# Repeated weight loads that pad every attention segment to three instruction pages

## The chip, the cores and the metric

The kernel runs on one core of one Trainium2 chip. Its time is the device time of that core in microseconds; three executions of the kernel before took 1864.36, 1864.82 and 1868.08 us, and the median, 1864.82 us, is what the changed kernel is compared with. The profiled execution took 1870.9 us.

A core has engines with instruction streams of their own. Here PE is the matrix engine (TensorE). It runs two kinds of instruction that matter: a weight load (LDWEIGHTS, shown as PEld), which puts the stationary operand into the array, and a matmul, which streams the moving operand through it. DVE is the vector engine, ACT the activation engine, POOL and SP further ones.

## The reference

Four layers follow each other on 2048 rows of 512 numbers: attention with a recurrent memory, a gated MLP, and the same two again, each with a layer norm before it and the residual added after it. What matters here is the attention, which goes over 64 segments of 32 rows, one after the other:

```python
mem = mem0                                        # 8 rows of memory
for s in range(n_seg):                            # 64 segments of 32 rows
    xs = x[:, s * seg_len:(s + 1) * seg_len, :]
    h = jnp.concatenate([mem, xs], axis=1)        # 40 rows of 512
    q = jnp.einsum('btd,dhe->bhte', h, Wq)        # 32 heads of 128
    k = jnp.einsum('btd,dhe->bhte', h, Wk)
    v = jnp.einsum('btd,dhe->bhte', h, Wv)
    scores = jnp.einsum('bhqe,bhke->bhqk', q, k) * scale
    scores = jnp.where(mask[None, None], scores, -1000000000.0)
    p = _softmax(scores, axis=-1)
    o = jnp.einsum('bhqk,bhke->bhqe', p, v)
    o = jnp.einsum('bhte,hed->btd', o, Wo)
    mem = o[:, :M, :]                             # the memory of the next segment
    outs.append(o[:, M:, :])
```

A segment needs the memory that the one before it leaves, so the 128 segments of the two attention layers form a chain.

## The kernel before

All work of a segment on PE is a fixed list. Two helpers issue most of it. `mm_chunk` makes 16 matmuls of 512 columns (4 steps of the contraction `kt`, in each 4 column groups `cg` of 32 columns that work side by side in the array), each with its own weight load; the program therefore holds 32 instructions per chunk. `wo_pass` makes 128 matmuls of 128 columns, which is 256 instructions.

```python
def mm_chunk(ps, lhs, rhs, kts=range(KT)):
    for kt in kts:
        for cg in range(4):
            nc.tensor.matmul(ps[32 * cg:32 * cg + 32, :], lhsT=lhs(kt, cg), rhs=rhs(kt, cg),
                             start=(kt == 0), stop=(kt == KT - 1), tile_position=(0, 32 * cg))

def wo_pass(po, lhs, heads=range(H)):
    for h in heads:
        n = h // 8 * 8 + 2 * (h % 4) + h // 4 % 2
        for cg in range(4):
            nc.tensor.matmul(po[32 * cg:32 * cg + 32, 0:128], lhsT=lhs[:, n, :], rhs=wo_rhs(h, cg),
                             start=(h == 0), stop=(h == H - 1), tile_position=(0, 32 * cg))
```

The order inside a segment, with the parts that are not on PE cut away (... marks a cut):

```python
def segment(s, fill, spare1, spare2, tail):
    ...
    r0 = qk(0)                    # one mm_chunk, then ScalarE copies PSUM to r0
    r2 = qk(2)
    qk_T(0, r0)                   # VectorE turns the rows
    r1 = qk(1)
    qk_T(2, r2)
    r3 = qk(3)
    qk_T(1, r1)
    ...
    scores(0)                     # 32 small matmuls for both score halves together
    qk_T(3, r3)
    ...
    v_mm(0, psV[0][:, 0, :])      # one mm_chunk
    fill()
    close(0)
    nc.vector.tensor_copy(VA[:, 0]..., psV[0][:, 0, :])
    scores(1)                     # needs qk_T(3)
    close(1)
    ...
    v_mm(1, psV[1][:, 0, :])
    fill()
    ...                           # psM: 4 matmuls
    pv(0)
    pv(1)                         # 32 matmuls for both
    ...                           # psD: 8 matmuls
    fill()
    ...
    wo_pass(pw, uT_cur)           # 128 matmuls
    ...
    build_hA(s + 1, pw)           # the next segment's input, from pw
    ...
    fill()
```

`fill()` takes the next piece of work that has no hurry and puts it where PE would wait: in the segments with `s % 4` of 1, 2 and 3 a part of the projections of the block of 128 rows to come (8, 8, 16 and 32 instructions in the four places of a segment), in those with `s % 4 == 0`, from the fifth block on, a part of an output projection (2, 2, 4 and 8 instructions). Without the fills a segment is 600 instructions on PE: 128 for the four qk chunks, 64 for the two v chunks, 64 for the scores, 8 for psM, 64 for pv, 16 for psD and 256 for the Wo pass.

Of the kernel before, what the change touches and what calls it, by code (L numbers as in the profile page):

```python
# [16 lines left out]
KT = 4  # L17
# [6 lines left out]
FF = 1376  # L24
FH = 688
LN_EXP_SET = 6
FCH = [(0, 128), (128, 128), (256, 128), (384, 128), (512, 128), (640, 48)]
ORDERED = {mybir.EngineType.PE, mybir.EngineType.DVE, mybir.EngineType.Activation}

# [75 lines left out]
def _ln_exp_table(nc):  # L105

    nc.scalar.add_instruction(mybir.InstLoadActFuncSet(name=nc.get_next_instruction_name(), engine=mybir.EngineType.Activation,
                                                       act_func_set_id=LN_EXP_SET, ins=[], outs=[]))

# [114 lines left out]
def b_block(tc, c, rows, front, xd, MV_out, RS_out, w_sp, w_out, S, first, out_final=None):  # L224
# [4 lines left out]
    with ExitStack() as ctx:  # L229
# [116 lines left out]
        def turn_u(t):  # L346
            pT = one.tile([P, 1024], BF16, name="pT")
            for fc, (f0, fsz) in enumerate(FCH):
                nc.tensor.transpose(pT[0:fsz, fc * P:(fc + 1) * P], u[t][:, f0:f0 + fsz], ident_bf[:])
# [4 lines left out]
        def finish(t):  # L354
            py = one.tile([P, DM], F32, name="py")
            for fc, (f0, fsz) in enumerate(FCH):
                nc.tensor.matmul(py[:], lhsT=uT[t][0:fsz, fc, :], rhs=w_out_sb[0:fsz, fc, :], start=(fc == 0), stop=(fc == 5))  # L357
# [33 lines left out]
def kernel(  # L391
# [55 lines left out]
    for blk in range(2):  # L447
        a_block(tc, c, rows, front, MV[0], RS[0], MV[1], RS[1], wqkv, A_Wo, S, first=(blk == 0))
        b_block(tc, c, rows, front, xd, MV[0], RS[0], B_w_sp, B_w_out, S, blk == 0, out_final=out2 if blk == 1 else None)
# [26 lines left out]
def a_block(tc, c, rows, front, MV_in, RS_in, MV_out, RS_out, wqkv, Wo, S, first):  # L476
    nc = tc.nc
    NSEG = S // SEG
    NB = S // P
# [3 lines left out]
    with ExitStack() as ctx:  # L483
# [33 lines left out]
        def qk_rhs(j, kt, cg):  # L517
            W_sb = Wq_sb if j < 2 else Wk_sb
            return W_sb[:, kt, :].rearrange("p (r gs i eb el) -> p r eb i gs el", r=2, gs=4, i=4, eb=4)[:, j % 2, cg]

        def v_rhs(r, kt, cg):
            return Wv_sb[:, kt, 2048 * r + 512 * cg:2048 * r + 512 * cg + 512]
# [1 line left out]
        def wo_rhs(h, cg):  # L524
            return Wo_sb[:, h, :].rearrange("p (kt g el) -> p g kt el", kt=4, g=4)[:, cg]

        def mm_chunk(ps, lhs, rhs, kts=range(KT)):

            for kt in kts:
                for cg in range(4):  # L530
                    nc.tensor.matmul(ps[32 * cg:32 * cg + 32, :], lhsT=lhs(kt, cg), rhs=rhs(kt, cg),  # L531
                                     start=(kt == 0), stop=(kt == KT - 1), tile_position=(0, 32 * cg))

# [23 lines left out]
        def b_units(tb, early=False):  # L557
            bs = blk_state[tb]

            for k, j in enumerate((0, 2, 1, 3, 4, 5)):  # L560
                ps = (accA if k % 2 == 0 or not early else accB).tile([P, 512], F32, name="psb")
                for kts in (((0,), (1,), (2, 3)), ((0, 1, 2, 3),))[k % 2]:
                    mm_chunk(ps, lambda kt, cg: bs["hB"][:, kt, :],
                             lambda kt, cg: qk_rhs(j, kt, cg) if j < 4 else v_rhs(j - 4, kt, cg), kts)
                    if kts[-1] != KT - 1:
                        yield

                def out(j=j, ps=ps):
                    if j >= 4:
                        nc.scalar.copy(bs["VB"][:, j - 4].rearrange("p i e -> p (i e)"), ps[:])  # L570
                        return
                    r = rowp.tile([P, 512], BF16, name="rowsB", bufs=2)
                    nc.scalar.copy(r[:], ps[:])  # L573
                    turns.append(lambda: nc.vector.transpose(
                        out=bs[("QTB", "KTB")[j // 2]][:, j % 2].rearrange("p a b -> p (a b)"), in_=r[:]))

                copies.append(out)
                yield
# [65 lines left out]
        def store_o(s, pw, eng):  # L644
# [2 lines left out]
            nc.scalar.copy(o_sb[:], pw[:, 0:128])  # L647
            eng.dma_start(o_d[SEG * (s - 1):SEG * s, :].rearrange("r (cg c) -> cg r c", cg=4), o_sb[:])

        def segment(s, fill, spare1, spare2, tail):  # L650
            tb, j4 = s // 4, s % 4
            st = seg_state.pop(s)
            QQ, KTB, VB = st["QQ"], st["KTB"], st["VB"]
            KA = KAr[s % 2]
            VA = vsp.tile([P, 2, 4, DH], BF16, name="VA")
            hA_cur = hA[s % 2]
# [5 lines left out]

            def qk(j):
                ps = (accB if j < 2 else accA).tile([P, 512], F32, name="psm")
                mm_chunk(ps, lambda kt, cg: hA_cur[:, kt, :], lambda kt, cg: qk_rhs(j, kt, cg))
                r = rowp.tile([P, 512], BF16, name="rows", tag="rowsQK", bufs=4)
                nc.scalar.copy(r[:], ps[:])  # L667
                return r
# [2 lines left out]
                nc.vector.transpose(out=QQ[:, j % 2, :, 0:32] if j < 2 else KA[:, j % 2], in_=r[:])  # L671

            def v_mm(r, ps):
                mm_chunk(ps, lambda kt, cg: hA_cur[:, kt, :], lambda kt, cg: v_rhs(r, kt, cg))

            def ends(q):

# [43 lines left out]
            def tok_out(r):  # L721
# [4 lines left out]
                                        in1=Rr[:, :, :, 24:32], op=ALU.mult)  # L726

            r0 = qk(0)
            r2 = qk(2)
            qk_T(0, r0)  # L730
# [3 lines that stand above are left out]
# [3 lines left out]
            qk_T(3, r3)  # L737
            psV = [attO[r].tile([P, 2, 512], F32, name="psV") for r in range(2)]
            v_mm(0, psV[0][:, 0, :])
            fill()  # L740
            close(0)
            nc.vector.tensor_copy(VA[:, 0].rearrange("p i e -> p (i e)"), psV[0][:, 0, :])
            scores(1)
            close(1)
            spare1()
            v_mm(1, psV[1][:, 0, :])
            fill()
            nc.scalar.copy(VA[:, 1].rearrange("p i e -> p (i e)"), psV[1][:, 0, :])  # L748
# [56 lines left out]
        for s in range(NSEG):  # L805
# [21 lines left out]
            def tail():  # L827
# [11 lines left out]
                if due and (j4 != 3 or tb + 2 >= NB):  # L839
                    ys.append(due.pop(0))  # L840
                    rows.y_load(ys[0], first, nc.sync)

            segment(s, lambda: next(more, None), spare1, spare2, tail)
        pw = accB.tile([P, 512], F32, name="pw")
        wo_pass(pw, uT[NSEG % 2])
# [47 lines left out]
```

The softmax here doesn't subtract the row's maximum and nothing guards it: scores larger than these inputs give would overflow.

## Time and profile before

| | |
|---|---|
| time, median of 3 | 1864.82 us |
| span of the profiled execution | 1870.9 us |
| PE busy | 1745.0 us (93%) |
| weight loads busy (overlap the matmuls) | 1007.2 us (54%) |
| DVE / ACT busy | 1156.5 us (62%) / 1112.3 us (59%) |
| PE instructions in the built program | 87,231 (43,596 weight loads, 43,596 matmuls, 39 others) |

In the views below a line of a group reads: source line, engine, operation, output and inputs by the program's names, shape, count; then busy time in us and the mean duration of one in ns; then the idle time of the engine just before them, and what ended most of it. "issue" stands where an engine waited for nothing that the profile shows. The chain of waits is the work that ended last, followed back from the end of the kernel; its lines read start, length, what.

An instruction takes 64 bytes, and the profile lists the transfers that bring instructions to the engines as a queue of their own: for one queue 340 packets and 5.57 MB, so 16.4 KB each, which is 256 instructions. The text calls such a packet a page, and the place in an instruction stream where one page ends and the next begins a page edge.

### The profile page before, as it was taken

What the parts mean: (1) busy time and instruction counts of PE and PEld (TensorE: products, weight loads), DVE (VectorE), ACT (ScalarE), POOL (GpSimd) and SP (SyncE); (2) the same over time, 40 slices, a digit from 0 to 9 for tenths busy, and PEclk for the clock granted to TensorE, in tenths of its full rate; (3) what the DMA queues carried; (4) which work ended last, traced back from release to release, by engine and by line L of the source; (5) the groups of instructions that cost most, each with busy time, mean ns of one, the idle gap of its engine ahead of it and who ended that gap; (6) DMA issues with size and microseconds to landing.
All of it is one profiled execution on the core that took longest, in us unless ns stands there. A gap on an engine that the chain in (4) does not pass through costs nothing.

```text
span 1870.9 us, 94288 instructions
## 1 busy us (share of the span) xinstructions
PE 1745.0 (93%) x43572; PEld 1007.2 (54%) x43596; DVE 1156.5 (62%) x2700; ACT 1112.3 (59%) x2074; POOL 137.1 (7%) x289
## 2 busy tenths in 40 slices
PE   2999999999999999889989999999999999998898
PEld 1555555555555555545545555555555555554455
DVE  1666666676667666674446666666766676665822
ACT  1666666766666666562036666666666666665600
POOL 5000000000000000032010000000000000001200
PEclk8999999999999999999989999999999999999999
DMA  9100000021002111277940000001210121114685
GB/s 348 48 19 20 20 19 17 20 72 38 19 16 71 42 26 37 80 159 166 206 134 21 21 21 21 22 21 32 80 35 21 28 88 39 29 47 112 155 181 135
DMA packets 189267, 125.80 MB, mean 67 GB/s; under 512 B 135896, under 2 KB 164328, under 8 KB 188872
## 3 DMA queue, kind: packets, MB, share of 16 engines
q1 hardware_dynamic: 167016, 71.01, 16.1%
q0 software_dynamic: 10560, 34.07, 5.6%
q10 hardware_dynamic: 11296, 14.70, 2.6%
q8 instruction: 340, 5.57, 1.2%
q14 instruction: 55, 0.45, 0.1%
HBM read 59.29 MB, written 33.56 MB: 50 GB/s over the span
## 4 chain that ended last, share of the span: by engine, by line
PE 85%; DMA 5%; DVE 4%; issue 3%; ACT 2%; POOL 1%; SPq 0%; ACTq 0%; DVEq 0%; POOLq 0%
PE psm L531 24%; PE pw L586 12%; PE psV L531 12%; PE psb L531 9%; PE pg L329 7%; PE psS L688 5%; PE psO L711 4%; PE pwB L598 4%; PE py L357 2%; PE psD L763 2%; DMA Wo_sb<-in_A_Wo_dram 2%; PE pz L263 1%; PE psM L753 1%; DMA uT<-u 1%; PE psM L754 1%
## 5 line engine op out<-in xcount | busy, mean ns | idle before, releaser
L531 PEld LDWEIGHTS <-hA 128*32 128x32 bf16 x12288 | 305.5, 96 | 316.9 <-DVE hA L642 47.8
L667 ACT CAST rows<-psm 128x512 bf16<-128x512 f32 x512 | 300.1, 586 | 198.4 <-PE psm L531 198.4
L586 PE MATMUL pw<-Wo_sb,uT 128*32 128x128 bf16 x16640 | 267.0, 220 | 40.6 <-issue 31.5
L531 PE MATMUL psm<-Wq_sb,hA 128*32 128x512 bf16 x4096 | 277.6, 384 | 12.8 <-DVE hA L642 9.3
L586 PEld LDWEIGHTS <-uT 128*32 128x32 bf16 x16640 | 236.1, 97 | 88.9 <-DVE uT L773 47.8
L531 PE MATMUL psm<-Wk_sb,hA 128*32 128x512 bf16 x4096 | 272.3, 382 | 0.5 <-ACT rowsB L573 0.5
L531 PE MATMUL psV<-Wv_sb,hA 128*32 128x512 bf16 x4096 | 268.0, 382 | 0.0
L671 DVE STREAM_TRANSPOSE QQ<-rows 128x512 bf16<-128x512 bf16 x256 | 182.0, 711 | 88.8 <-ACT rows L667 87.7
L723 DVE TENSOR_TENSOR uT<-psO,Rt 128x384 bf16<-128x384 f32 x256 | 138.5, 541 | 119.2 <-ACT Rt L779 119.0
L692 ACT ACTIVATE E<-psS 128x448 bf16<-128x448 f32 x256 | 139.9, 547 | 117.8 <-PE psS L688 117.8
L671 DVE STREAM_TRANSPOSE KA<-rows 128x512 bf16<-128x512 bf16 x256 | 181.8, 710 | 40.4 <-ACT rows L667 38.9
L773 DVE TENSOR_TENSOR uT<-psO,Rm 128x128 bf16<-128x128 f32 x256 | 62.4, 286 | 163.7 <-PE psD L763 163.7
L779 ACT ACTIVATE Rt<-Rt 128x512 f32<-128x512 f32 x256 | 157.4, 629 | 4.1
L329 PE MATMUL pg<-z2n,wspT 128*128 128x344 bf16 x1024 | 154.8, 309 | 1.0 <-DVE u L337 1.0
L688 PEld LDWEIGHTS <-KA 128*64 128x64 bf16 x2048 | 79.8, 113 | 106.0 <-DVE KA L671 105.2
L771 ACT ACTIVATE Rt<-psD 128x1024 f32<-128x1024 f32 x128 | 131.2, 1025 | 6.0
L531 PEld LDWEIGHTS <-hB 128*32 128x32 bf16 x3072 | 77.8, 97 | 97.0 <-issue 25.4
L329 PEld LDWEIGHTS <-wspT 128*128 128x128 bf16 x1024 | 97.9, 98 | 54.2 <-issue 7.8
L695 DVE TENSOR_TENSOR E<-E,maskN 128x448 bf16<-128x448 bf16 x256 | 95.2, 372 | 41.7 <-ACT E L692 41.7
L531 PE MATMUL psb<-Wq_sb,hB 128*32 128x512 bf16 x1024 | 89.9, 391 | 26.2 <-DVE hB L546 26.2
L688 PE MATMUL psS<-QQ,KA 128*64 128x80 bf16 x2048 | 109.9, 208 | 1.1
L748 ACT CAST VA<-psV 128x512 bf16<-128x512 f32 x128 | 75.0, 586 | 56.5 <-PE psV L531 56.5
(147 smaller groups left out, 2216.1 us busy)
## 6 DMA issues: line engine op xcount, KB each, us to landing
Wo_sb<-in_A_Wo_dram POOLq DMA_DIRECT2D x8, 1024.0 KB, 13.6
xs<-xd ACTq DMA_DIRECT2D x32, 256.0 KB
o_d<-o_sb SPq DMA_DIRECT2D x126, 64.0 KB
y_o<-o_d SPq DMA_DIRECT2D x24, 256.0 KB
xd<-y_o SPq DMA_DIRECT2D x22, 256.0 KB
Wq_sb<-in_A_Wq_dram POOLq DMA_DIRECT2D x8, 512.0 KB, 6.8
Wk_sb<-in_A_Wk_dram POOLq DMA_DIRECT2D x8, 512.0 KB, 10.7
Wv_sb<-in_A_Wv_dram POOLq DMA_DIRECT2D x8, 512.0 KB, 11.4
```

Source lines behind the costliest of these rows:

```text
L329: nc.tensor.matmul(pg[t][:, k, 0:344], lhsT=wsp[t][:, st, :], rhs=z2n[:, st, 344 * k:344 * k + 344], start=(st == 0), stop=(st == NT - 1))
L531: nc.tensor.matmul(ps[32 * cg:32 * cg + 32, :], lhsT=lhs(kt, cg), rhs=rhs(kt, cg), start=(kt == 0), stop=(kt == KT - 1), tile_position=(0, ...
L586: nc.tensor.matmul(po[32 * cg:32 * cg + 32, 0:128], lhsT=lhs[:, n, :], rhs=wo_rhs(h, cg), start=(h == 0), stop=(h == H - 1), tile_position ...
L667: nc.scalar.copy(r[:], ps[:])
L671: nc.vector.transpose(out=QQ[:, j % 2, :, 0:32] if j < 2 else KA[:, j % 2], in_=r[:])
L688: nc.tensor.matmul(pS[64 * g:64 * g + 64, i, c0:80 if K is KA else 112], lhsT=K[:, r, n:n + 2, :].rearrange("p h k -> p (h k)"), rhs=q if ...
L692: nc.scalar.activation(out=E[:, r], in_=pS, func=ACT.Exp, scale=scale)
L695: nc.vector.tensor_tensor(out=E[:, r], in0=E[:, r], in1=maskN[:, j4, :].unsqueeze(1).to_broadcast([P, 4, 112]), op=ALU.mult)
L723: nc.vector.tensor_tensor(out=hview(uT_nxt[:], r, 8, 32), in0=oview(r, 8, 32), in1=Rr[:, :, :, 0:24], op=ALU.mult)
L748: nc.scalar.copy(VA[:, 1].rearrange("p i e -> p (i e)"), psV[1][:, 0, :])
L771: nc.scalar.activation(out=Rt[:], in_=psD[:], func=ACT.Ln)
L779: nc.scalar.activation(out=rt, in_=rt, func=ACT.Exp, scale=-1.0)
```

## The change

The changed kernel issues weight loads a second, third, ... time, with the same weights and no matmul of their own, until every segment is 768 PE instructions long: 3 pages of 256. As a Wo pass has 256 instructions, every Wo pass contains exactly one page edge; before, its place moved from segment to segment, because a segment of 600 instructions and its fills is not a whole number of pages. With 768 it stays at the same place. The loads go before the 16 matmuls of `qk(3)` and of `v_mm(0)`, spread evenly, half in each chunk. `again_of` counts them: 168 less the fills that lie between this Wo pass and the one before it, so 104 in the segments with `s % 4` of 2 and 3, 136 (or 128) in the others, and up to 168 in a layer's last block, which has hardly any fills; the first segment of each layer gets fewer, by `FILL_AHEAD`, which sets where the edge falls. In the built program every Wo pass inside the chain of segments has it at the same place, about 97 instructions in.

```diff
+PE_PAGE = 256
+SEGMENT_PE = 600
+FILL_AHEAD = ((0, 0, 0, 98), (0, 0, 0, 95))
...
-        def mm_chunk(ps, lhs, rhs, kts=range(KT)):
+        def mm_chunk(ps, lhs, rhs, kts=range(KT), again=0):
 
             for kt in kts:
                 for cg in range(4):
+                    k = 4 * kt + cg
+                    for _ in range(again * (k + 1) // 16 - again * k // 16):
+                        nc.tensor.ldweights(lhs(kt, cg), tile_position=(0, 32 * cg))
                     nc.tensor.matmul(ps[32 * cg:32 * cg + 32, :], lhsT=lhs(kt, cg), rhs=rhs(kt, cg),
                                      start=(kt == 0), stop=(kt == KT - 1), tile_position=(0, 32 * cg))
...
+        def fills_of(s):
+
+            if s < 0:
+                return FILL_AHEAD[not first]
+            if s % 4 == 0:
+                return (2, 2, 4, 8) if s // 4 > 3 else (0, 0, 0, 0)
+            return (8, 8, 16, 32) if s // 4 + 1 < NB else (0, 0, 0, 0)
+
+        def again_of(s):
+
+            return 3 * PE_PAGE - SEGMENT_PE - fills_of(s - 1)[3] - sum(fills_of(s)[:3])
+
         def segment(s, fill, spare1, spare2, tail):
             tb, j4 = s // 4, s % 4
+            again = again_of(s)
...
-                mm_chunk(ps, lambda kt, cg: hA_cur[:, kt, :], lambda kt, cg: qk_rhs(j, kt, cg))
+                mm_chunk(ps, lambda kt, cg: hA_cur[:, kt, :], lambda kt, cg: qk_rhs(j, kt, cg), again=again // 2 if j == 3 else 0)
...
-                mm_chunk(ps, lambda kt, cg: hA_cur[:, kt, :], lambda kt, cg: v_rhs(r, kt, cg))
+                mm_chunk(ps, lambda kt, cg: hA_cur[:, kt, :], lambda kt, cg: v_rhs(r, kt, cg), again=again - again // 2 if r == 0 else 0)
```

In the built program that is 15,167 weight loads more (58,763 in place of 43,596), 102,398 PE instructions in place of 87,231. Two more things stand there that the diff does not show: each extra load increments PE's semaphore, and in the two chunks that hold extra loads each of the 16 matmuls does so too, where before only the last one of a chunk did. No other engine's work changes.

## The prediction

> **What bounds the kernel now.** I read the page first, then the chain of waits in one stretch, then all that the Wo line waits for, then the timeline of one segment.
>
> ```profile
> PE 1745.0 (93%) x43572; PEld 1007.2 (54%) x43596; DVE 1156.5 (62%) x2700; ACT 1112.3 (59%) x2074; POOL 137.1 (7%) x289
> ...
> q8 instruction: 340, 5.57, 1.2%
> ...
> PE 85%; DMA 5%; DVE 4%; issue 3%; ACT 2%; POOL 1%; SPq 0%; ACTq 0%; DVEq 0%; POOLq 0%
> ...
> L531 PEld LDWEIGHTS <-hA 128*32 128x32 bf16 x12288 | 305.5, 96 | 316.9 <-DVE hA L642 47.8
> ...
> L688 PEld LDWEIGHTS <-KA 128*64 128x64 bf16 x2048 | 79.8, 113 | 106.0 <-DVE KA L671 105.2
> ```
>
> PE carries 85% of the chain; no other engine or DMA comes near. 3% of the chain, 56 us of 1870.9, is "issue": PE had nothing to wait for and yet did nothing. Two passes of the chain show what that is:
>
> ```profile
> 646.33 1.68 PE pw L586 x119
> 648.01 0.90 issue
> 648.92 0.34 PE pw L586 x9
> ...
> 658.62 1.90 PE pw L586 x128
> ```
>
> One Wo pass stops for 0.90 us after 119 of its 128 matmuls, another runs through in 1.90 us. The pass's own view says how often:
>
> ```profile
> L586 PEld LDWEIGHTS <-uT x16640: 92/97/150, 52.8 to 1713.1; 128*32 128x32 bf16 x199
> ...
>   issue: 72.3, 91
> ```
>
> (72.3 us counts loads and matmuls, so most stalls twice.) Laying the program's PE list beside the trace's weight-load starts explains it. Gaps over 300 ns that no semaphore accounts for lie at instruction 194 or 195 and whole multiples of 256 after it: page edges. In Wo passes whose edge is 0 to 168 instructions in, the loads take 1.70 us from first to last, always; beyond about 170 nearly all stop at the edge. Counted over the attention, 65 stalls hold up the loads for 61 us in all: 43 in Wo passes (41 us), 22 in the qk chunks just after one (20 us). Where the edge before was under 2.3 us away, so that waiting surely ended the interval (26 cases), edge to resumption took 2.3 to 4.0 us, mean 3.1, spread 0.4. So a page needs about 3.1 us after the previous edge, and edges closer in time than that cost the difference. A Wo pass eats a page in 1.7 us; a qk chunk takes 0.87 us for 32 instructions.
>
> The segments agree: the stretch from one Wo pass to the next takes at best 11.30, 11.23, 11.10 and 11.10 us for the four segments of a block, and 0.5 us more on average. Between stalls PE is saturated; nothing else is to be had.
>
> **What the Trainium skill says.** "Runtime: NRT & Kernel Launch", section Instruction fetch mechanics: instructions come in 16 KiB blocks of 256, fetched while the current one runs, and the cost of an edge is "mostly hidden". The block size agrees (5.57 MB over 340 packets); "hidden" fails where 256 instructions take under 3 us. "TensorE: Matmul & The Clock Gate", section LDWEIGHTS (loading the stationary operand), gives columns / 1.2 ns, so 27 ns for 32 columns; the trace contradicts it: a Wo pass does 128 such loads in 1.80 us, 14 ns each, and 64 columns take 113 ns against 96, so 17 ns for 32 columns more. The same page, section The mechanism, says loads are pulled ahead of running matmuls; the trace agrees (loads for the next step begin 2 ns after the matmul whose weights they replace). The same page, section The cost: per-tile semaphore tail, says that increments of a semaphore serialise at 26.3 ns each. Nothing in the trace of before shows it, since only one matmul of a chunk increments there.
>
> **The change part by part.**
>
> Removed: up to 56 us of stalls. New stalls: with 768 instructions a segment has three edges, where before it had about 2.6. I placed the new edges on the clean timing of before (extra loads at no time): from Wo to the qk chunks 3.85 or 4.42 us, from there into scores(1), or the fills and loads just before it, mostly 3.54 or 3.51 us, but 3.09 us in 22 segments and 2.0 to 2.9 us in some 20 (first and last blocks of a layer), and from there to the next Wo edge mostly 3.71 us. Against 3.1 +- 0.4 us the 22 cost 0.2 us each (4 us), the 20 some 0.5 (10), all others a few hundredths (6): 20 us. Net gain 56 - 20 = 36 us, so 1829 us if the extra loads are free.
>
> Added, the loads: 15,167 / 128 = 118 a segment, 59 in each of two chunks, 15 in each step of 216 ns beside the four that belong there. At the Wo pass's 14 ns, 19 loads need 266 ns, 50 ns over the 216 of the matmuls. Times 4 steps, 2 chunks and 128 segments: 51 us. This is a lower bound on the load path's rate, since in a Wo pass the matmuls (128 columns, 56 ns for a group of four) set the pace as well; loads for different column groups start 3 to 4 ns apart, and two loads of one group have been 15 ns apart at the start of a chunk. With 15 ns inside a group and 3.4 ns between groups a chunk with 52 extra loads just fits, one with 64 to 68 is 150 to 210 ns over: about 26 us. I take 30 us, and 1859 us in all.
>
> Added, the increments: 59 + 16 = 75 in a chunk of 0.87 us. At 26.3 ns they take 1.97 us. The signal that qk(3) is ready would come some 0.9 us late, and it has no slack:
>
> ```profile
> 664.02 1.05 PE L531 MATMUL psm<-Wk_sb,hA 128*32 128x512 bf16 x16
> ...
> 665.11 0.59 ACT L667 CAST rows<-psm 128x512 bf16<-128x512 f32 x1 [0.28 <-PE psm L531]
> ...
> 665.73 0.71 DVE L671 STREAM_TRANSPOSE KA<-rows 128x512 bf16<-128x512 bf16 x1 [0.15 <-ACT rows L667]
> ...
> 666.24 0.39 PE L531 MATMUL psb<-Wq_sb,hB 128*32 128x512 bf16 x4
> ...
> 666.56 0.11 PEld L688 LDWEIGHTS <-KA 128*64 128x64 bf16 x2 [0.42 <-DVE KA L671]
> ```
>
> The last qk chunk ends at 665.07; the ACT copy, the DVE transpose (to 666.44) and the second score loads at 666.56 follow at once, while PE has just finished its fill. 0.9 us late is 0.9 us lost, 118 us over 128 segments, so 1829 + 118 = 1947 us.
>
> **The rivals.**
>
> (1) Loads are nearly free: repeated loads overlap the streaming matmuls, increments do not queue. About 1829 us. For it: loads run ahead by design, the four groups accept them 3 to 4 ns apart, and chunk steps leave 200 of 216 ns without a load. Against: repeated loads of one group without a matmul between occur nowhere in this trace.
>
> (2) The load path fills up, increments do not matter: 1845 to 1885 us, my central case. The fetch gain is mostly handed back.
>
> (3) The increments queue, or a repeated load has to wait for the matmul that still uses the array: a new wait takes the place of the removed one, at scores(1) or inside the two chunks. 1900 to 1980 us for the increments. For it: the skill's figure and the tight chain above. If each repeated load waited for the whole of the one before it (96 ns), 118 of them would be 11 us a segment and the time would nearly double; against that speak loads of one group 15 ns apart.
>
> **Range and chances.** I give (1) 0.2, (2) 0.45, (3) 0.35. Even (1) lands near 1829, while 2% faster begins at 1827.5 and needs the residual stalls to be hidden too; so faster gets 0.14. Within 2% (to 1902) takes the rest of (1), all of (2): 0.48. Slower 0.38. The middle of this is 1860 us; 8 times in 10 I expect 1820 to 1980.
>
> **What would show each step right or wrong.** Wo passes: all should run through in 1.70 us of loads, with no "issue" in them; a single stall of 0.5 us or more in most passes would mean I have the edge or its mechanism wrong. "issue" on the chain should fall from 3% to about 1%. The fetch queue should carry some 399 packets. qk(3) and v_mm(0): their 16 matmuls should start over 0.65 us (3 steps of 216 ns) if loads are hidden, 0.8 to 1.1 us in case (2). Case (3) would show as ACT's copy of qk(3) starting late after the chunk's last matmul, or as PE weight loads at scores(1) waiting for DVE KA far over 0.42 us. Wrong in everything would be a fetch that depends on anything but the time since the last edge, such as other DMA traffic, or a chunk that slows several times over.

## The result, and the profile after

| | before | after |
|---|---|---|
| median of the comparison | 1865.62 us (4 runs) | 2098.56 us (4 runs, 2090.28 to 2101.63) |
| ratio, 95% interval | 1 | 1.1232 [1.1202, 1.1262] |
| first to last Wo pass, layers 1 and 2 | 732.9 and 737.5 us | 841.2 and 841.5 us |
| the rest of the profiled execution | 400.5 us | 405.9 us |

The change makes the kernel 12% slower, 233 us. The profiled execution after took 2088.6 us; 212 of its 218 us over before lie in the two attention stretches.

The page after, the same rows as before (column meanings are the same; the program's lines have moved, L531 is now L537, L586 is L592 and L688 is L707; the added loads are L536):

```profile
PE 1946.2 (93%) x43572; PEld 1372.9 (66%) x58763; DVE 1162.5 (56%) x2700; ACT 1109.9 (53%) x2074; POOL 137.3 (7%) x289
...
q8 instruction: 400, 6.55, 1.3%
...
PE 57%; ACT 11%; DVE 11%; PEld 10%; issue 7%; DMA 3%; SPq 1%; POOL 0%; ACTq 0%; DVEq 0%; POOLq 0%
...
L686 ACT CAST rows<-psm 128x512 bf16<-128x512 f32 x512 | 300.2, 586 | 377.6 <-PE L536 262.6
...
L536 PEld LDWEIGHTS <-hA 128*32 128x32 bf16 x15167 | 357.1, 93 | 23.3
...
L690 DVE STREAM_TRANSPOSE KA<-rows 128x512 bf16<-128x512 bf16 x256 | 181.8, 710 | 230.5 <-ACT rows L686 229.6
```

PE is as busy as before by share (93%), yet its part of the chain fell from 85 to 57%: ACT and DVE have come onto it. The ACT copies of the qk chunks now idle for 262.6 us until an added weight load (L536) lets them go, and the transpose behind them for 229.6 us. A row that puts ACT's wait down to a weight load shows that the loads' increments go to the semaphore on which ACT waits.

"issue" on the chain rose from 3 to 7%, where the prediction said about 1%. These are not page stalls: in the changed kernel the chain runs over the weight loads of the qk chunks, and the time between the loads of one step and the next, in which the matmuls go on, counts as "issue":

```profile
708.33 0.11 issue
708.44 0.11 PEld L537 x4
708.54 0.11 issue
```

What the change was meant to do in the Wo passes, it did. The Wo line's own view after:

```profile
L592 PEld LDWEIGHTS <-uT x16640: 92/97/97, 53.5 to 1928.8; 128*32 128x32 bf16 x199
...
  issue: 6.3, 8
```

"issue" ahead of Wo's loads and matmuls went from 72.3 us to 6.3 us; of the Wo passes of the attention one stalls, where 43 did.

The timeline of one segment (start us, length, engine, what; in brackets the idle time before it and its releaser) shows the price:

```profile
710.81 1.19 PE L537 MATMUL psm<-Wk_sb,hA 128*32 128x512 bf16 x16
...
712.58 1.69 PE L537 MATMUL psV<-Wv_sb,hA 128*32 128x512 bf16 x16
...
713.21 0.59 ACT L686 CAST rows<-psm 128x512 bf16<-128x512 f32 x1 [1.58 <-PE L536]
...
713.83 0.71 DVE L690 STREAM_TRANSPOSE KA<-rows 128x512 bf16<-128x512 bf16 x1 [1.46 <-ACT rows L686]
...
714.59 0.11 PEld L707 LDWEIGHTS <-KA 128*64 128x64 bf16 x2 [0.44 <-DVE KA L690]
...
715.66 0.55 ACT L711 ACTIVATE E<-psS 128x448 bf16<-128x448 f32 x1 [1.43 <-PE psS L707]
```

qk(3) ends at 712.00. Before, ACT's copy followed within 0.04 us; here it starts 1.21 us after that end, and the transpose (which turns the rows into KA) and the second score loads wait for it. That is the signal the prediction spoke of, 0.3 us later still than it said. A second late signal it did not speak of: ACT takes up the second scores (E, L711) 1.07 us after their first load, 714.59 to 715.66. In the segment of before that the prediction shows, that was 0.49 us, from 666.56 to

```profile
667.05 0.54 ACT L692 ACTIVATE E<-psS 128x448 bf16<-128x448 f32 x1 [0.91 <-PE psS L688]
```

The third thing is that v_mm(0) itself takes 1.69 us where a chunk took 1.05. The starts of PE's instructions show how (loads in ns of the trace; own and added loads together, matmuls left out):

```
qk(3), at first:   710809 710817 710824 710826 710832 710840 710841 710847 710855 710856 710862 710863 710871
qk(3), at the end: 711364 711394 711424 711454 711488 711518 711548 711578 711608
v_mm(0):           712602 712632 712662 712696 712726 712756 712786 712820 712850 712880 712910
```

The first loads of qk(3) follow each other by 1 to 8 ns. After some 55 increments, 0.55 us into the chunk, one goes out in 30 ns (34 where a matmul stands between), and v_mm(0) begins at that pace. So increments do not just arrive late: they hold back the loads and matmuls that carry them.

The trace also records when each increment of PE's semaphore takes effect. In the whole execution they follow each other by 30 ns 15,167 times, which is the number of the added loads, and by 34 or 35 ns 3,970 times; the matmuls have 3,840 increments more than before. At 711.36 us, when the hold sets in, 58 increments had been issued since the first added load and 10 had come out, so 48 had been let ahead. Those of qk(3) are all out at 713.18 us, just before ACT's copy, and those of v_mm(0) at 715.45 us; that of the second scores follows at 715.64, and ACT starts on them at 715.66. So both late signals stand in one row of increments. (In v_mm(0) the hold begins with only 25 outstanding, and at 713.2 us, when those of qk(3) are out, some 25 loads go out fast once more; why is open.)

### The profile page after: what moved, and what is told of

It is laid out like the page before. It is cut to its first block, busy times and chain, and to the rows that moved or that the text cites. A ratio compares the mean times of both kernels' runs of the same rounds, so it can differ in the third digit from the quotient of the medians.

```text
span 2088.6 us, 109455 instructions
## 1 busy us (share of the span) xinstructions
PE 1946.2 (93%) x43572; PEld 1372.9 (66%) x58763; DVE 1162.5 (56%) x2700; ACT 1109.9 (53%) x2074; POOL 137.3 (7%) x289
## 4 chain that ended last, share of the span: by engine, by line
PE 57%; ACT 11%; DVE 11%; PEld 10%; issue 7%; DMA 3%; SPq 1%; POOL 0%; ACTq 0%; DVEq 0%; POOLq 0%
PE psm L537 13%; PE psS L707 9%; PE pg L332 7%; PE psV L537 7%; PE pw L592 5%; PEld L537 4%; PEld L536 4%; PE psO L730 4%; ACT Rt L790 3%; ACT E L711 3%; PE psb L537 3%; PE pwB L604 3%; DVE E L714 2%; PE py L360 2%; DVE KA L690 2%
## 5 line engine op out<-in xcount | busy, mean ns | idle before, releaser
L537 PEld LDWEIGHTS <-hA 128*32 128x32 bf16 x12288 | 501.8, 94 | 195.7 <-DVE hA L648 50.6
L686 ACT CAST rows<-psm 128x512 bf16<-128x512 f32 x512 | 300.2, 586 | 377.6 <-PE L536 262.6
L537 PE MATMUL psV<-Wv_sb,hA 128*32 128x512 bf16 x4096 | 382.9, 381 | 0.3
L536 PEld LDWEIGHTS <-hA 128*32 128x32 bf16 x15167 | 357.1, 93 | 23.3
L537 PE MATMUL psm<-Wk_sb,hA 128*32 128x512 bf16 x4096 | 309.7, 381 | 0.5 <-ACT rowsB L579 0.5
L690 DVE STREAM_TRANSPOSE KA<-rows 128x512 bf16<-128x512 bf16 x256 | 181.8, 710 | 230.5 <-ACT rows L686 229.6
L537 PE MATMUL psm<-Wq_sb,hA 128*32 128x512 bf16 x4096 | 268.8, 381 | 11.3 <-DVE hA L648 9.7
L592 PEld LDWEIGHTS <-uT 128*32 128x32 bf16 x16640 | 233.7, 97 | 50.5 <-DVE uT L792 46.4
L592 PE MATMUL pw<-Wo_sb,uT 128*32 128x128 bf16 x16640 | 256.7, 219 | 8.7 <-DVE uT L792 5.3
L711 ACT ACTIVATE E<-psS 128x448 bf16<-128x448 f32 x256 | 140.0, 547 | 209.4 <-PE psS L707 209.4
L761 DVE CAST VA<-psV 128x512 bf16<-128x512 f32 x128 | 88.6, 692 | 112.7 <-PE psS L707 112.5
L707 PEld LDWEIGHTS <-KA 128*64 128x64 bf16 x2048 | 100.2, 111 | 73.8 <-DVE KA L690 37.6
L707 PE MATMUL psS<-QQ,KA 128*64 128x80 bf16 x2048 | 138.8, 207 | 7.6 <-DVE KA L690 1.0
L537 PEld LDWEIGHTS <-hB 128*32 128x32 bf16 x3072 | 96.1, 97 | 73.5 <-DVE hB L552 26.1
L537 PE MATMUL psb<-Wq_sb,hB 128*32 128x512 bf16 x1024 | 103.7, 393 | 27.2 <-DVE hB L552 27.2
```

What stands on the lines that cost most here:

```text
L536: nc.tensor.ldweights(lhs(kt, cg), tile_position=(0, 32 * cg))
L707: nc.tensor.matmul(pS[64 * g:64 * g + 64, i, c0:80 if K is KA else 112], lhsT=K[:, r, n:n + 2, :].rearrange("p h k -> p (h k)"), rhs=q if ...
L711: nc.scalar.activation(out=E[:, r], in_=pS, func=ACT.Exp, scale=scale)
```

## The experiments

Theory I: the increments are the cost. Each of the 15,167 added loads has one, and so has each of the 32 matmuls of the two chunks, where before it was one in a chunk. Rival II: the loads themselves. Rival III: page edges that now fall worse. All ratios are to the kernel before, run beside on the same chip (medians 1876.38, 1874.41 and 1874.48 us in the three sets). In the sums "floor" is the shortest time from one Wo pass to the next in the fifth to the last but one block, for segments with s % 4 = 0, 1, 2, 3 (before: 11.30, 11.23, 11.10, 11.10 us; after: 13.60, 13.67, 12.85, 12.85).

### The same loads without increments

The added loads are copied into PE's finished list, without a semaphore, at the places where the changed kernel has them. Number and place of instructions, and so the page edges, are the changed kernel's.

```diff
-                    for _ in range(again * (k + 1) // 16 - again * k // 16):
-                        nc.tensor.ldweights(lhs(kt, cg), tile_position=(0, 32 * cg))
-                    nc.tensor.matmul(...)
+                    mm = nc.tensor.matmul(...)
+                    REPEATS[mm.ins.name] = again * (k + 1) // 16 - again * k // 16
...
+                if isinstance(i, mybir.InstMatmult) and REPEATS.get(i.name):
+                    for _ in range(REPEATS[i.name]):
+                        out.insert(held, copy_load(ld, mybir, ...))
```

> The changed kernel, instruction for instruction the same repeated weight loads in the same places, but none of them increments a semaphore, and the matmuls of the two chunks increment as before (only the last of a chunk). Theory I (the increments are the cost, the loads themselves nearly fit beside the matmuls): 1830 to 1865 us, so below or about the kernel before; qk(3) and v_mm(0) take 0.65 to 0.9 us from first to last matmul start. Theory L (the repeated loads fill the load path, or wait for running matmuls): still above 2000 us. If both share the cost: 1900 to 2000 us. In all cases every Wo pass has its page edge 97 instructions in, and none should stall.

Measured: 1867.23 us, ratio 0.9943 [0.9923, 0.9962], just above the range of Theory I. Floors 11.48, 11.41, 11.27, 11.27 us; the attention stretches 726.4 and 731.8 us. The timeline of one of its segments, from qk(3) on:

```profile
572.64 1.13 PE L536 MATMUL psm<-Wk_sb,hA 128*32 128x512 bf16 x16
...
573.82 0.59 ACT L686 CAST rows<-psm 128x512 bf16<-128x512 f32 x1 [0.36 <-PE psm L536]
...
574.13 1.08 PE L536 MATMUL psV<-Wv_sb,hA 128*32 128x512 bf16 x16
574.44 0.71 DVE L690 STREAM_TRANSPOSE KA<-rows 128x512 bf16<-128x512 bf16 x1 [0.24 <-ACT rows L686]
```

ACT again follows qk(3) at once, and v_mm(0) takes 1.08 us. The increments are what differs between the two programs; they make 841.2 + 841.5 - 726.4 - 731.8 = 224.5 us. The loads cost 0.17 to 0.18 us of a segment's floor, 22 us in 126 segments. And since the stretches are 1470.4 - 1458.2 = 12.2 us shorter than before in spite of that 22, some 34 us of stalls have gone by this sum. This run has the changed kernel's page edges and none of its 12%, so Rival III is out as a cause.

### Fewer loads, edges that drift

```diff
-            return 3 * PE_PAGE - SEGMENT_PE - fills_of(s - 1)[3] - sum(fills_of(s)[:3])
+            return 32
```

> The changed kernel with 32 repeated loads a segment (one for each matmul of the two chunks) in place of 118, so the edges move again as before. Each chunk then has 32 increments. Theory I: 32 increments at the 30 ns seen in the changed kernel are 0.96 us against 0.87 us of matmuls, so a signal some 0.1 us late, twice a segment: 10 to 40 us slower than before, 1875 to 1905 us, with page stalls as before. Theory L (loads): 8 loads in a step of 216 ns are less than the 15 that a Wo pass takes in that time, no cost: 1860 to 1872 us. If each increment cost its time wherever it stands, 64 a segment would cost 1.9 us, 2100 us.

Measured: 1899.78 us, ratio 1.0121 [1.0103, 1.0139]. With 16 loads and 32 increments a chunk the floors are 11.41, 11.45, 11.32, 11.32 us, 0.11 to 0.22 over before (16 loads a chunk included), and 44 Wo passes stall for 41.3 us, as before (43, 39.2 us). Padding that does not fix the edge saves nothing.

### The edge at a bad place

Bare loads as above, but 143 more ahead of the first segment, so that the edge falls late in every Wo pass.

```diff
-FILL_AHEAD = ((0, 0, 0, 98), (0, 0, 0, 95))
+FILL_AHEAD = ((0, 0, 0, -45), (0, 0, 0, 95))
```

> As the first of these, without increments, but with 143 more loads in the first segment, so that the page edge lies 210 instructions into every Wo pass in place of 97. If the place of the edge matters as the trace of before suggests (stall where the edge is beyond about 170), nearly every Wo pass stalls some 0.6 to 0.9 us: 75 to 115 us more than the first run. If the place does not matter (the stalls come from something else that moved with the segments): the same as the first run.

Measured: 1955.97 us, ratio 1.0416 [1.0392, 1.044], 89 us over the run with the edge early in the pass. The waits view (us in total, times, longest) and the chain of waits in one pass:

```profile
PEld L592 <- issue: 111.8, 126, 2.0
```

```profile
603.10 1.47 PE pw L592 x104
604.56 1.27 issue
605.84 0.52 PE pw L592 x24
```

Now 121 of 126 passes stop for over 0.3 us, always after 104 matmuls: 208 instructions, the place the edge was moved to. The idea behind the change is right and its placing in the Wo pass good.

### The increments spread over six chunks

```diff
+            share = [again * (n + 1) // 6 - again * n // 6 for n in range(6)]
...
-  ... qk_rhs(j, kt, cg), again=again // 2 if j == 3 else 0)
+  ... qk_rhs(j, kt, cg), again=share[(0, 2, 1, 3).index(j)])
...
-  ... v_rhs(r, kt, cg), again=again - again // 2 if r == 0 else 0)
+  ... v_rhs(r, kt, cg), again=share[4 + r])
```

> The same 15,167 loads, each with its increment, spread evenly over all six chunks of a segment (about 20 loads and 16 matmul increments in each, 36 a chunk; 214 increments a segment in place of 150 plus four), page edges where the changed kernel has them. Theory R (a chunk of 0.87 us takes about 28 increments for nothing and each further one costs some 22 ns; from the changed kernel's two chunks and the run with 16 loads a chunk): 8 more than free in each of six chunks, about 0.2 us a chunk, 0.9 to 1.2 us a segment over the run with bare loads, so a Wo-to-Wo floor of 12.2 to 12.7 us and a ratio of 1.055 to 1.075. Theory S (every increment costs its 22 to 30 ns wherever it stands): more increments in all, so slower than the changed kernel, over 1.12. Theory T (only the sum of increments counts against the whole segment, 214 x 30 ns = 6.4 us in 11.2 us): as with bare loads, 0.99 to 1.00.

Measured: 2026.06 us, ratio 1.0805 [1.0782, 1.0828]; floors 13.01, 13.02, 12.31, 12.31 us. Less than with two chunks, though there are 60 more increments in a segment; more than Theory R's range. S and T are out. A segment with s % 4 = 2 at work:

```profile
631.24 1.22 PE L537 MATMUL psm<-Wk_sb,hA 128*32 128x512 bf16 x16
...
632.42 1.06 PE L537 MATMUL psm<-Wq_sb,hA 128*32 128x512 bf16 x16
...
633.48 1.07 PE L537 MATMUL psm<-Wk_sb,hA 128*32 128x512 bf16 x16
```

Chunks that followed each other in 0.87 us now start 1.18 and 1.06 us apart. R's "22 ns each beyond the free ones" was too small: at 30 ns, 29 increments fit into 0.87 us. Segments with s % 4 = 1 have 128 added loads, 37 increments a chunk, 8 too many: 6 x 8 x 30 ns = 1.44 us, against 1.61 measured over the bare loads; those with s % 4 = 2 or 3 have 104, 33 a chunk: 6 x 4.3 x 30 ns = 0.78 us against 1.04.

### All of the loads in one chunk

```diff
-  ... qk_rhs(j, kt, cg), again=again // 2 if j == 3 else 0)
+  ... qk_rhs(j, kt, cg), again=0)
...
-  ... v_rhs(r, kt, cg), again=again - again // 2 if r == 0 else 0)
+  ... v_rhs(r, kt, cg), again=again if r == 0 else 0)
```

> The changed kernel with all of its incrementing loads in v_mm(0), none in qk(3): the same 15,167 loads and page edges, but 1,920 increments fewer, since the matmuls of qk(3) no longer carry one each. Theory L (PE lets out one increment in 30 ns, and what a stretch has more than fits its time delays what follows): 120 to 144 increments take 3.6 to 4.3 us from the start of v_mm(0), 5.0 to 5.2 us after the Wo pass, so v_mm(1) starts at 8.7 to 9.4 us, where it was 7.84 to 8.63 with the loads in two chunks; 0.8 us more in a segment, ratio 1.16 to 1.185, slower than the changed kernel. Theory N (only the number of increments counts, or only the late signal of qk(3), which is now on time): not slower than the changed kernel, 1.06 to 1.12.

Measured: 2185.12 us, ratio 1.1661 [1.1638, 1.1685]. Fewer increments, and 4% slower than the changed kernel: Theory N is out.

```profile
689.66 0.59 ACT L686 CAST rows<-psm 128x512 bf16<-128x512 f32 x1 [0.28 <-PE psm L537]
...
690.03 2.56 PE L537 MATMUL psV<-Wv_sb,hA 128*32 128x512 bf16 x16
690.28 0.71 DVE L690 STREAM_TRANSPOSE KA<-rows 128x512 bf16<-128x512 bf16 x1 [0.15 <-ACT rows L686]
...
692.74 0.23 PE L707 MATMUL psS<-QQ,KA 128*64 128x80 bf16 x2
...
693.39 1.13 PE L537 MATMUL psV<-Wv_sb,hA 128*32 128x512 bf16 x16
...
694.11 0.54 ACT L711 ACTIVATE E<-psS 128x448 bf16<-128x448 f32 x1 [3.41 <-PE psS L707]
```

Here the signal of qk(3) is on time: DVE has KA ready at 690.99. PE gets to the second scores only at 692.74, because it has itself been held in v_mm(0). A late signal of qk(3) is not needed for the loss. The signal of the second scores is late here too: ACT takes them up 1.37 us after their first load.

The starts of the chunks in a segment with s % 4 = 2, in us after the last Wo load (medians of 32 segments), put the runs side by side:

| | qk(3) | v_mm(0) | second scores | ACT's E of them | v_mm(1) | next Wo | increments from qk(3) through v_mm(0) |
|---|---|---|---|---|---|---|---|
| before | 3.64 | 4.99 | 6.18 | 6.67 | 6.56 | 9.40 | 2 |
| after | 3.64 | 5.41 | 7.43 | 8.50 | 7.84 | 11.15 | 136 |
| bare loads | 3.64 | 5.13 | 6.36 | 6.85 | 6.74 | 9.58 | 2 |
| all in v_mm(0) | 3.64 | 5.11 | 7.81 | 9.18 | 8.46 | 11.83 | 121 |

136 x 30 ns = 4.08 us; after, v_mm(1) starts 4.20 us after qk(3). 120 x 30 = 3.6 us; with all in v_mm(0), v_mm(1) starts 3.35 us after it, a little earlier than expected: in the segment shown 18 increments are still outstanding then. What is between (scores, the fill) is hidden under that. The next Wo pass comes 2.65 to 2.73 us after E in all four, so in the two with increments the time follows from when their row is out. Two chunks cost less than one, with 15 increments more, because their row begins 1.47 us earlier, at qk(3). After, the second scores start 0.06 us after KA is ready (7.37): the hold of PE in v_mm(0) is covered there, and the loss goes by the two late signals. With all in v_mm(0) KA is ready at 6.07, and PE is held past it; whether that hold costs anything beyond the late E was not separated.

### Bare loads, shared out by page intervals

The bare loads left about 22 us of stalls, counted against the shortest gap at the same place; not in that sum are the last three segments of each layer, which all stop for 1.0 to 1.6 us in v_mm(0). 24 segments stop at an edge in the fills just before the Wo pass (2.9 to 3.2 us after the edge before), others in the qk chunks. Here the same number of bare loads is divided over qk(1), qk(3), v_mm(0) and v_mm(1), by kind of segment, so that two edges stand 3.3 us or more apart.

```diff
+        def share_of(s):
+            if s % 4 > 1 and s // 4 + 1 < NB:
+                return 6, 0
+            if s % 4 == 0:
+                return (7, 45) if s // 4 < 4 else (3, 6)
+            ...
-            again = again_of(s)
+            early, late = share_of(s) if s else (0, 0)
+            again = again_of(s) - early - late
...
-  ... again=again // 2 if j == 3 else 0)
+  ... again=again // 2 if j == 3 else early if j == 1 else 0)
...
-  ... again=again - again // 2 if r == 0 else 0)
+  ... again=again - again // 2 if r == 0 else late)
```

> Loads without increments, as in the run with bare loads, but shared out over qk(1), qk(3), v_mm(0) and v_mm(1), by the fills of the segment, so that the two edges between one Wo pass and the next stand at least 3.3 us from each other and from those of the Wo passes. The number of instructions of a segment and the place of the Wo pass's edge stay. Theory P (a page needs about 3.1 us after the edge before, and nothing else stalls): the stalls left with bare loads, about 17 us in the qk chunks and 8 us at the end of the fills in segments with s % 4 = 0, fall below 5 us in all; ratio to the kernel before 0.982 to 0.988, floors of the segments unchanged. Rival (the stalls left come from something other than the interval, or the repeated loads cost more where no other load gap hides them): ratio 0.992 to 0.998, as with bare loads.

Measured: 1856.80 us, ratio 0.9896 [0.9874, 0.9919], the best of all: 1% under before, 12% under the changed kernel. The stretches take 721.8 and 721.0 us, 27.6 us less than before's. The waits view of the bare loads, then of this run (us, times, longest):

```profile
PEld L536 <- issue: 39.8, 85, 5.4
...
PEld L604 <- issue: 21.2, 48, 0.9
```

```profile
PEld L536 <- issue: 33.2, 71, 5.3
PEld L604 <- issue: 18.5, 48, 0.4
```

The 24 stalls in the fills (L604) are gone: its longest wait fell from 0.9 to 0.4 us. But 51 of 378 edges still hold the loads for over 0.3 us, 18 us in all, where under 5 were expected. 34 of these are among 108 edges that PE reached 3.3 to 3.5 us after the one before (from the first load behind one edge to the last ahead of the next). So a page's time is no constant of 3.1 us: at one distance some edges hold the loads and others do not. In the kernel before 2 of 12 at that distance did, too few to say whether it happens more often where all edges are close (three in 11.3 us). That fetching falls behind over several pages would fit; it was not tried by itself.

Outside the stretches this run took 414.3 us. The kernel before was profiled once more, on another chip, to see what that part takes there:

> The kernel before once more, for its stretches on this chip: from first to last Wo pass of a layer 732 to 738 us, as in its first profile; what lies outside these stretches (407 to 414 us in the runs with bare loads, 400.5 in the first profile of before) 404 to 412 us here, if it is the chip and not the padding that makes it longer.

It took 731.3 and 735.1 us in the stretches and 403.8 us outside (1871.93 us in all). So some 10 us of the 24 gained inside went outside, in the MLP and its surroundings. Why was not tried; among the kernels with the changed kernel's number of PE instructions that part took 405.9 to 415.3 us. It is not the chip alone: the next run, on the chip of this repeat, took 409.3 us there.

### No extra load in a chunk's first step

```diff
-   ... again * (k + 1) // 16 - again * k // 16
+   ... again * (k - 3) // 12 - again * (k - 4) // 12 if k > 3 else 0
```

(and 36 in place of 25 early loads in one kind of segment, so that its edges stay where they were.)

> Bare loads shared out over the chunks as in the balanced run, but none in the first step of a chunk: the extra loads stand in the last three of its four steps only. In the balanced run the first matmul of v_mm(0) starts 0.12 us later after Wo than before and the Wo-to-Wo floors are 11.48, 11.38, 11.23 and 11.23 us, 0.13 to 0.18 over those before; some 12 extra loads 7 ns apart stand ahead of a chunk's first matmul, where no matmul hides them. Theory F (the whole cost of a bare load is this start of a chunk): floors within 0.05 us of the kernel before, some 0.1 us less than balanced in each of 126 segments, ratio 0.981 to 0.986. Rival (the loads cost wherever they stand, since 20 loads 7 ns apart need 140 of a step's 216 ns and delay the matmuls): floors as in the balanced run or up to 0.05 us more, 0.988 to 0.992.

Measured: 1857.05 us, ratio 0.992 [0.9894, 0.9947], the same as the balanced run. Both theories are half right. The floors with s % 4 = 1, 2, 3 fell to 11.23, 11.12, 11.12 us, within 0.02 us of before; v_mm(0) starts at 5.00 us again. So in these segments the cost of a bare load lies at the start of a chunk, where no matmul hides it. (s % 4 = 0 stayed at 11.48; why is open.) But the time did not follow: 100 edges stall in place of 51, for some 32 us in place of 18, among them 61 of the 130 at a distance of 3.3 to 3.5 us. The loads went faster and stood at the edge instead.

## Why the prediction was wrong

1860 us with a range to 1980 was said, 2098.56 came.

**Fetch.** Said: 56 us of stalls removed, 20 new, so 36 us gained. Bare loads: 34 us gained, and of the 61 us of stalls that the prediction counted some 22 are left, with the last segments' besides. The edge's place was right (one Wo pass of the changed kernel stalls), the fetch packets too (399 said, 400 seen). A sign against the model came as well: the time since the last edge does not decide alone, since at 3.3 to 3.5 us some edges stalled and others did not.

**The loads.** Said: 51 us at 14 ns a load, 26 by the four groups, 30 taken. Measured: 22 us, and in three of the four kinds of segment these only at a chunk's start. The 14 ns from the Wo pass were no load rate: bare loads mostly go out 1 to 10 ns apart in a chunk.

**The increments: the step that failed.** "The signal that qk(3) is ready would come some 0.9 us late, and it has no slack", "118 us over 128 segments, so 1829 + 118 = 1947 us". The kind was right, and the place: ACT's copy late, the second scores waiting. The size was not: 224.5 us in the runs in place of 118, for two reasons. The signal of qk(3) is later than 0.9 us: in the segments of the table ACT's copy starts 1.31 us later than before (6.04 against 4.73 us after the Wo loads), and 1.63 us in those with s % 4 of 0 and 1, which have more loads. An increment takes 30 to 35 ns, not 26.3, and the first comes out only 0.2 us after the chunk's first matmul. And the term stopped at that signal. The increments of v_mm(0) stand in the same row, ahead of the signal of the second scores, which makes ACT's E later by another 0.58 us: 1.25 us from the second scores starting late and 0.58 from their own signal are 1.83 us at E (8.50 against 6.67), and 1.75 us at the next Wo pass. The term also took PE as going on while its increments queue; v_mm(0) and the run with all loads in it show that PE is held, loads and matmuls alike, though in the changed kernel the wait for KA covers that hold. So the rate and its reach were both needed.

**The weights.** Case (3) got 0.35 and (2) 0.45, and the range ended at what (3) alone would make by its first term. Against (3) there was nothing in the trace; there was only no sight of it, since before one matmul of a chunk increments. The Trainium skill, "TensorE: Matmul & The Clock Gate", section The cost: per-tile semaphore tail, gave 26.3 ns; the trace after shows 30 to 35. A stated figure that makes 75 increments last over twice as long as the work they belong to deserved to be the central case. The chances do not quite add up either: the rest of (1) and all of (2) are 0.06 + 0.45 = 0.51, not 0.48.

**Rivals.** (1), loads nearly free, and (2), where they hand back most of the fetch gain, are worlds without increments; the bare loads were made into one, and there (2) holds: 34 us gained, 22 handed back, 0.6% left.

## What to carry to other kernels

Count the semaphore increments of each stretch and multiply by 30 ns (35 for a matmul's) before adding instructions that are meant to be free: if that exceeds the stretch's time, every later signal of the engine waits behind them, and with some 50 outstanding the engine itself is held. Filler belongs in the finished list without semaphores, behind a chunk's first step. And a page edge is placed by time: keep it away from the late part of a dense pass and from its neighbours (over 3.7 us after the one before, 3 of 134 edges stalled in the balanced run and 5 of 123 in the last), and count that padding brings more pages.

## What the runs showed of the hardware that was not expected

- For a row of PE instructions that each increment a semaphore, an increment takes 30 ns on a weight load and 34 or 35 ns on a matmul: 15,167 and 3,970 gaps after, 4,095 and 3,842 in the run with 32 loads a segment (4,096 loads and 3,840 matmul increments added). At most 55 to 58 were outstanding in the runs with the most; PE is held then, weight loads and matmuls alike. 32 in a chunk of 0.87 us, in two chunks, cost 0.11 to 0.22 us a segment, with the 16 loads of each.
- A repeated weight load of 32 columns without semaphore mostly goes out 1 to 10 ns after the one before it, though the trace gives each 92 to 98 ns, and behind the first step of a chunk it costs 0.02 us a segment or less in three of the four kinds.
- Edges reached under 2.5 us after the one before: 49 of 54 stalled in before, 100 of 100 with the edge late in Wo. At 3.3 to 3.5 us it was 2 of 12 in before, 61 of 130 in the last run with bare loads.
